# Two tile sizes in the first expert layer: 348 rows, and 294 for what is left of an expert

## The chip, the core and the metric

The program runs on one core of a Trainium2 chip. The core has a matmul engine (TensorE, PE in the rows, with its weight loads as PEld), a vector engine (VectorE, DVE), an activation engine (ScalarE, ACT), a general engine (GpSimd, POOL) and a sequencer that issues most of the transfers (SyncE, SP). The metric is the device time of one execution in microseconds, taken as the median of several runs.

## The reference

Three layers follow one another: a squared-ReLU attention, and two layers in which every row goes through one of eight small networks ("experts"). The change is in the first expert layer. Cut to that:

```python
N, D, E, F = (9984, 256, 8, 1024)
out = x.copy()
xc = x[x @ w_skip > 0]
logits = xc @ w_gate
e_idx = np.argmax(logits, axis=1)
gate_w = softmax(logits)[np.arange(len(xc)), e_idx]
for e in range(E):
    mask = e_idx == e
    h = np.maximum(xc[mask] @ w1[e], 0.0)
    y[mask] = gate_w[mask, None] * (h @ w2[e])
out[do_compute] = xc + y
```

The second expert layer takes all 9984 rows, picks an expert for each in the same way, and has the same two matmuls. The inputs are fixed. Counted with the reference, the experts of the first layer get 628, 689, 640, 488, 610, 684, 607 and 613 rows, 4959 in all; in the second layer two experts get 5042 and 4942.

## The kernel before

**Stages.** The attention runs first, up to about 715 us. While it runs, each row of the result is written into the list of its expert in memory, by indirect transfers. Then come the tiles of the first expert layer, about 714 to 1005 us, and those of the second, up to the end. A tile of the first layer is 348 rows of one expert's list, 116 partitions times 3 groups (`P1, G1`, `T1`); one of the second layer is 512 rows.

**A turn.** One tile is worked on in one turn (`Moe.turn`, `Moe.work`). Its PE work is eight steps `h0` to `h7` (`hidden`, L833: six matmuls each, the two weight halves times the two halves of the rows, since every number is split into a high and a low part), and eight steps `o0` to `o7` (`Moe1.out_part`, L939: six matmuls each). After each `h` step ACT makes the high part `hh` (L835) and DVE the low part `hl` (L836); three PSUM buffers `ph` serve the `h` steps in turn. Behind each step hang hooks, by a table named `PLAN`; the order on each engine is the order in which the hooks are written.

**What the hooks do.** Into a turn are woven (a) the loads for the next turn, 2 MB of weights and the rows; (b) the splitting of weights in high and low parts, `w2` by ACT and POOL (L715) at `h2` to `h5`, `w1` by ACT and DVE (`zB`, L717) at `o1` to `o5`; (c) the transposes of the next tile's rows (`x_transposed`, L816, with ACT's `mxh` and DVE's `mxl` L821) at `o0` and `o2`, through one PSUM buffer; (d) the steps of `after`, which finish the tile before: its result is copied out, the gate of the second layer is computed from it (`logits_t` L962 behind `h2`, ACT's copies `mlt` L968, `logits` L988 behind `h4`, the pick of the expert, which ends with the one-hot `ohbb` of L1003), the places in the lists are ranked (`ranks`, L1010, behind `o0`), and the rows are transposed back (L975) and scattered into the lists of the second layer (`m1.send`, L737, on POOL).

**Sixteen turns.** An expert of 488 to 689 rows takes two tiles, so there are sixteen. Turns 1 to 3 are written out and take the first 348 rows of experts 0, 1 and 2, which are full by then. A table then says which expert and which rows each further tile has (`Table.make`, in steps spread over turns 1 and 2; it ends in `spread`, one matmul of `diag` by ones, L650, and three copies of it on DVE). All engines read the count `n`, here 12, from SBUF (`count`, L663) and go into a loop (L1279) of twelve turns; turn 16 is written out behind it and loads for the second layer. At the end of a loop there is a barrier: SP waits for the transfers that the loop issued, POOL gathers, and all engines are released.

## Time and profile before

| | us |
|---|---|
| median of 3 runs | 1476.23 (1475.93 to 1477.01) |
| the profiled execution | 1476.05 |
| its span, first to last instruction | 1474.2 |
| PE busy in the span | 1459.5 |
| granted PE clock, mean | 0.999 of full speed |

The profile is one execution. Times in its rows are microseconds from the span's start; the 1.85 us between the span and the execution's time are outside the instructions. A timeline row gives start, length, engine, line, operation, tiles and shapes, a count where equal instructions were merged, and in brackets how long the engine had been idle before it and what ended that. A length includes the engine's pipeline: matmuls that follow one another at 0.16 us have lengths of 0.32 us. So the pace is read from starts.

### The profile page before, as it was taken

To read this page: it belongs to the slowest core of one execution; us is meant where nothing else is said; L and a number is where in the kernel's file an instruction comes from. 1 tells how busy PE (TensorE), PEld (TensorE's weight loads), DVE (VectorE), ACT (ScalarE), POOL (GpSimd) and SP (SyncE) were. 2 spreads that over 40 slices of the span, in tenths; PEclk is the share of its full clock that TensorE was granted. 3 is DMA by queue.
4 is the path that set the end of the run, shared out by engine and by line. 5 is a ranking of instruction groups with operands and counts; after the bars stand their busy time and mean duration, and the time that the engine had idled before them with its cause. 6 is when DMAs were issued, how large, how long until landed. Compare 5 with 4: busy or idle time off the path is not lost. (4 is left out here: it accounts for less than half of the span.)

```text
span 1474.2 us, 35153 instructions
## 1 busy us (share of the span) xinstructions
PE 1459.5 (99%) x10985; PEld 1263.7 (86%) x10985; DVE 1070.8 (73%) x2540; ACT 946.6 (64%) x1721; POOL 509.8 (35%) x788
## 2 busy tenths in 40 slices
PE   9999999999999999999999999999999999999998
PEld 7988888888888888888889999998888888888886
DVE  8888888888888888787887777777555555555553
ACT  8877777777777787776556666654554545545453
POOL 2011111111111111111356556655535445354454
PEclk9999999999999999999999999999999999999999
DMA  6411211112111140011345655554433344334440
GB/s 231 180 41 56 80 38 42 44 59 73 37 43 44 58 145 31 29 61 45 99 140 182 184 185 179 180 173 131 172 133 129 132 153 140 132 129 132 154 140 28
DMA packets 46370, 161.00 MB, mean 109 GB/s; under 512 B 12118, under 2 KB 12821, under 8 KB 37056
## 3 DMA queue, kind: packets, MB, share of 16 engines
q1 hardware_dynamic: 29232, 124.57, 26.0%
q0 software_dynamic: 16896, 35.11, 6.8%
q8 instruction: 62, 1.02, 0.3%
q14 instruction: 36, 0.29, 0.1%
q10 hardware_dynamic: 144, 0.02, 0.0%
HBM read 124.57 MB, written 36.21 MB: 109 GB/s over the span
## 5 line engine op out<-in xcount | busy, mean ns | idle before, releaser
L350 PE MATMUL o<-ah,vh 64*128 64x512 f32 (+1 forms) x1560 | 313.6, 384 | 0.1
L350 PE MATMUL o<-al,vh 64*128 64x512 f32 (+1 forms) x1560 | 306.8, 383 | 0.0
L350 PE MATMUL o<-ah,vl 64*128 64x512 f32 (+1 forms) x1560 | 304.9, 382 | 0.0
L836 DVE SCALAR_TENSOR_TENSOR hl<-ph,hh 128x512 fp32r<-128x512 f32 (+1 forms) x288 | 176.3, 613 | 146.3 <-ACT hh L835 138.6
L715 POOL TENSOR_TENSOR w<-w2raw,w 128x256 fp32r<-128x256 f32 x282 | 198.5, 744 | 211.1 <-issue 188.4
L737 POOL DMA_INDIRECT lists<-r,ix x80 | 102.0, 1275 | 476.5 <-ACT t L310 246.5
L312 DVE TENSOR_TENSOR al<-t,ah 128x1024 fp32r<-128x1024 f32 (+2 forms) x201 | 239.9, 1193 | 19.0
L298 ACT ACTIVATE t<-s 128x1024 f32<-128x1024 f32 (+2 forms) x201 | 201.2, 1002 | 79.5 <-PE s L295 71.8
L835 ACT ACTIVATE hh<-ph 128x512 fp32r<-128x512 f32 (+1 forms) x288 | 155.6, 540 | 100.3 <-PE ph L833 92.7
L833 PE MATMUL ph<-mxh,zA 128*128 128x512 f32 (+1 forms) x576 | 209.3, 363 | 3.1 <-DVE hl L836 1.6
L310 ACT ACTIVATE t<-t 128x1024 f32<-128x1024 f32 (+2 forms) x201 | 208.1, 1036 | 5.7
L833 PE MATMUL ph<-mxh,zB 128*128 128x512 f32 (+1 forms) x576 | 207.0, 359 | 0.0
L833 PE MATMUL ph<-mxl,zA 128*128 128x512 f32 (+1 forms) x576 | 206.8, 359 | 0.0
L311 DVE CAST ah<-t 128x1024 fp32r<-128x1024 f32 (+2 forms) x201 | 136.9, 681 | 63.0 <-ACT t L310 59.7
L350 PEld LDWEIGHTS o<-ah,vh 64*128 64x128 f32 x1560 | 153.9, 184 | 28.0 <-DVE xs L363 0.5
L350 PEld LDWEIGHTS o<-al,vh 64*128 64x128 f32 x1560 | 154.0, 184 | 25.9 <-DVE al L312 0.2
L350 PEld LDWEIGHTS o<-ah,vl 64*128 64x128 f32 x1560 | 150.4, 184 | 25.9
L939 PE MATMUL o<-hh,w 128*128 128x348 f32 x512 | 124.8, 327 | 0.0
L833 PEld LDWEIGHTS ph<-mxh,zA 128*128 128x128 f32 x576 | 108.4, 188 | 19.0 <-DVE hl L836 3.1
L820 ACT CAST mxh<-m 128x512 fp32r<-128x512 f32 (+1 forms) x72 | 37.9, 526 | 134.6 <-PE m L816 83.4
L295 PE MATMUL s<-zA,zB 64*128 64x512 f32 (+1 forms) x400 | 123.9, 386 | 0.0
L295 PE MATMUL s<-zB,zA 64*128 64x512 f32 (+1 forms) x400 | 121.6, 387 | 0.0
(240 smaller groups left out, 3012.8 us busy)
## 6 DMA issues: line engine op xcount, KB each, us to landing
w1raw<-in_w SPq DMA_DIRECT2D x36, 1024.0 KB
w2raw<-in_w SPq DMA_DIRECT2D x36, 1024.0 KB
x_in<-lists SPq DMA_DIRECT2D x20, 536.0 KB
vraw<-in_v SPq DMA_DIRECT2D x20, 512.0 KB
ut<-in_uT SPq DMA_DIRECT2D x20, 512.0 KB
lists<-x_in POOLq DMA_DIRECT2D x16, 536.0 KB
x_cur<-lists SPq DMA_DIRECT2D x16, 351.8 KB
x_in<-lists SPq DMA_DIRECT2D x15, 351.8 KB
```

The lines of the kernel that those rows point to most:

```text
L295: nc.tensor.matmul(s[:, i, :n], w[p, k], x[p, q], start=(j == 0), stop=(j == 2))
L298: nc.scalar.activation(t[:, i, :n], s[:, i, :n], AF.Relu, scale=SCALE)
L310: nc.scalar.activation(t[:, i, :n], t[:, i, :n], AF.Square)
L311: nc.vector.tensor_copy(h[:, i, :n], t[:, i, :n])
L312: nc.vector.tensor_tensor(l[:, i, :n], t[:, i, :n], h[:, i, :n].bitcast(F32), op=ALU.subtract)
L350: nc.tensor.matmul(o[half][d][:, :n], w[p, d * 128:d * 128 + 128], x[p, :n], start=(u == 0 and j == at[0]), stop=(u == 9 and j == at[-1]),)
L715: lo_engine.tensor_tensor(l[:, c], src[:, c], h[:, c].bitcast(F32), op=ALU.subtract)
L737: i = tc.nc.gpsimd.indirect_dma_start(out=out, out_offset=bass.IndirectOffsetOnAxis(ap=ix, axis=0), in_=rows, in_offset=None, bounds_check ...
L833: nc.tensor.matmul(ps, w, x, start=(i == 0), stop=(i == len(mms) - 1))
L835: nc.scalar.activation(h, ps, AF.Relu)
L836: nc.vector.scalar_tensor_tensor(l, ps, 0.0, h.bitcast(F32), op0=ALU.max, op1=ALU.subtract)
L939: nc.tensor.matmul(self.y[d], w[:, dd], h[f], start=(f == 0 and i == 0), stop=(f == 7 and i == 2))
```

## The change

There is a third tile size, `P3 = 98` partitions times 3 groups, `T3 = 294` rows. The main table counts a tile of 348 only where more than 294 rows are left after the tiles before it. With the counts above, that is ten tiles of 348 (three of them in turns 1 to 3), and six of 294, for experts 0, 2, 3, 4, 6 and 7 (280, 292, 140, 262, 259 and 265 rows left); experts 1 and 5 have two of 348. A second object `s1`, which shares the tiles of `m1`, works the small tiles. It has a table of its own, made in eight hooks of turn 3 (`step3`, and the `spread` at `o7`). The first loop then has six turns, and behind it stand a written-out turn of 348, a written-out turn of 294, a second loop of four turns of 294, and a written-out turn of 294. There are still sixteen turns, and the weights are still loaded sixteen times. In `Scatter.group` the small POOL instruction ahead of a transfer reads another column.

```diff
+P3 = 98
+T1, T2, T3 = P1 * G1, P2 * G2, P3 * G1
...
+    def rest(self, nc, pool, k, m):
+        lists, self.T = self.lists, T3
+        self.lists = pool.tile([128, 5 * E + 1], F32, name=f"plan_lists{m}")
+        done = pool.tile([128, E], F32, name=f"done{m}")
+        nc.vector.tensor_scalar(done, self.nt, float(T1), None, op0=ALU.mult)
+        nc.vector.tensor_tensor(self.lists[:, 0:E], lists[:, 0:E], done, op=ALU.add)
+        nc.vector.tensor_copy(self.lists[:, E:3 * E], lists[:, E:3 * E])
+        yield
+        yield from self.make(nc, pool, k, lists[:, 3 * E:4 * E], done, None, m, T3, 0, 1, 2.0)
...
+    tiles = {T1: -(-N // T1), T2: -(-N // T2), T3: 1}
+    for T, least in ((T1, T3), (T2, 0), (T3, 0)):
+        k.steps[T] = const.tile([128, tiles[T]], F32, name=f"steps{T}")
+        iota(k.steps[T], tiles[T], T, least)
...
+    t3 = s1.table.rest(nc, sh.p, k, 3)
+    step3 = (lambda: next(t3, None),)
+    m1.turn(lambda: m1.next(-1), m1.after(plan.lim[:, 0, :, 1:2], lambda: 2 * N), {
+        **{at: [*hs] for at, hs in m1.PLAN.items()},
+        ("h", 2): [*m1.PLAN["h", 2], step3],
+        ("h", 3): [*m1.PLAN["h", 3], step3],
+        ("h", 7): [*m1.PLAN["h", 7], step3],
+        ("o", 3): [step3],
+        ("o", 4): [*m1.PLAN["o", 4], step3],
+        ("o", 5): [*m1.PLAN["o", 5], step3],
+        ("o", 6): [step3],
+        ("o", 7): [(lambda: s1.table.spread(nc, sh.ps_m, k),)],
+    })
     n = m1.table.count(nc)
     with tc.For_i(0, n, 1, iteration_sync=mode, head_align_engines=(mybir.EngineType.PE,)) as j:
         m1.send()
         m1.turn(lambda: m1.next(j), m1.finish(j))
     m1.send()
+    m1.turn(lambda: s1.next(-1), m1.finish(n))
+    m1.send()
+    last = m1.after(m1.table.lim[:, :, ds(n + m1.table.S, 1)], lambda: s1.table.row(nc, 0, T3), then=s1)
+    s1.turn(lambda: s1.next(0), last)
+    m1.send()
+    n = s1.table.count(nc)
+    with tc.For_i(0, n, 1, iteration_sync=mode, head_align_engines=(mybir.EngineType.PE,)) as j:
+        s1.send()
+        s1.turn(lambda: s1.next(j + 1), s1.finish(j + 1))
+    s1.send()
...
-    m1.turn(lambda: (m2, e2, ra), m1.finish(n))
+    s1.turn(lambda: (m2, e2, ra), s1.finish(n + 1))
```

On DVE, in turn 3 from `h2` to `h5`, this stands before the change (`hl` are the low parts of `h3`, `h4` and `h5`, L988 is the gate's logits):

```order
L966 COPY mlt<-m 16x116
L836 SCALAR_TENSOR_TENSOR hl_10867<-ph,hh_10859 128x348
L836 SCALAR_TENSOR_TENSOR hl_10868<-ph,hh_10860 128x348
L988 SCALAR_TENSOR_TENSOR m<-m,x_cur 116x8 x3
L836 SCALAR_TENSOR_TENSOR hl_10869<-ph,hh_10861 128x348
```

After the change the same stretch reads so (L602 to L625 are the first two steps of the new table):

```order
L988 COPY mlt<-m 16x116
L602 TENSOR_SCALAR done_11561<-nt_11201 128x8
L603 TENSOR_TENSOR plan_lists_11560<-plan_lists,done_11561 128x8
L604 COPY plan_lists_11560<-plan_lists 128x16
L851 SCALAR_TENSOR_TENSOR hl_10869<-ph,hh_10861 128x348
L621 TENSOR_TENSOR plan_lists_11560<-plan_lists,done_11561 128x8
L624 TENSOR_TENSOR over_11578<-plan_lists_11560,steps_107 128x8
L625 TENSOR_REDUCE nt_11579<-over_11578 128x8
L851 SCALAR_TENSOR_TENSOR hl_10870<-ph,hh_10862 128x348
L1010 SCALAR_TENSOR_TENSOR m<-m,x_cur 116x8 x3
L851 SCALAR_TENSOR_TENSOR hl_10871<-ph,hh_10863 128x348
```

Three small instructions stand ahead of the low part of `h3` and three ahead of that of `h4`.

On PE, at the end of turn 3 (the last matmuls of `o7`, the read of the count, the branch into the loop, the first matmul of `h0`), this stands before the change:

```order
L939 MATMUL o_10883<-hl_10871,w_10855 128x348
L663 TENSOR_LOAD n_i_11428
L1279 COMPARE_AND_BRANCH
L1279 ISA
L1279 UNCONDITIONAL_BRANCH
L1370 BRANCH_PREFETCH_HINT
L833 MATMUL ph<-mxh,zA_114 128x348
```

and this after it:

```order
L961 MATMUL o_10885<-hl_10873,w_10857 128x348
L665 MATMUL m<-diag_11753,ones_f 128x90
L678 TENSOR_LOAD n_i_11436
L1317 COMPARE_AND_BRANCH
L1317 ISA
L1317 UNCONDITIONAL_BRANCH
L1418 BRANCH_PREFETCH_HINT
L848 MATMUL ph<-mxh,zA_116 128x348
```

The matmul of the new table's `spread` stands between the last output matmul and the loop.

On PE, in the loop's turn behind `o2` (transposes back of the third group, then the second half of the next tile's rows), this stands before the change:

```order
L939 MATMUL o_10883<-hl_10866,w_10853 128x348
L975 ISA
L975 MATMUL m<-ident,yS 116x128 x2
L816 REGISTER_ALU
L816 MATMUL m<-ident,x_in 128x116 x3
L939 MATMUL o_10882<-hh_10859,w_10853 128x348
```

and this in the second loop after it:

```order
L961 MATMUL o_10885<-hl_10868,w_10855 128x294
L997 ISA
L997 MATMUL m<-ident,yS 98x128 x2
L831 REGISTER_ALU
L831 MATMUL m<-ident,x_in 128x98 x3
L961 MATMUL o_10884<-hh_10861,w_10855 128x294
```

Order and number of instructions are the same; the shapes are smaller.

## Rows read from the trace of the kernel before

**Rows 1.** The page: busy time of each engine, share of the span, instructions.

```profile
PE 1459.5 (99%) x10985; PEld 1263.7 (86%) x10985; DVE 1070.8 (73%) x2540; ACT 946.6 (64%) x1721; POOL 509.8 (35%) x788
```

**Rows 2.** Timeline of PE: first and last of runs of equal matmuls.

```profile
862.32 0.32 PE L833 MATMUL ph<-mxh,zA 128*128 128x348 f32 x1
...
865.02 0.33 PE L833 MATMUL ph<-mxh,zB 128*128 128x348 f32 x1
...
1239.70 0.39 PE L833 MATMUL ph<-mxh,zA 128*128 128x512 f32 x1
...
1248.99 0.40 PE L833 MATMUL ph<-mxh,zB 128*128 128x512 f32 x1
1249.23 0.39 PE L1107 MATMUL o<-w,hh 128*128 128x512 f32 x1
...
1253.04 0.40 PE L1107 MATMUL m<-w,hh 128*128 128x512 f32 x1
```

**Rows 3.** Timeline of PE in a turn of the loop, which starts at 862.32.

```profile
871.73 0.19 PE L1010 MATMUL m<-ohbb,tri 116*128 116x32 bf16 x1
...
874.83 0.52 PE L816 MATMUL m<-ident,x_in 116*128 116x116 f32 x3
...
879.94 0.32 PE L833 MATMUL ph<-mxh,zA 128*128 128x348 f32 x1
```

**Rows 4.** Timeline of ACT in that turn.

```profile
866.08 0.51 ACT L968 COPY mlt<-m 16x116 f32<-16x116 f32 x2
...
868.04 0.46 ACT L835 ACTIVATE hh<-ph 128x348 fp32r<-128x348 f32 x1
```

**Rows 5.** Timeline of DVE in that turn.

```profile
868.61 0.52 DVE L836 SCALAR_TENSOR_TENSOR hl<-ph,hh 128x348 fp32r<-128x348 f32 x1 [0.39 <-ACT hh L835]
...
871.31 0.18 DVE L1003 TENSOR_TENSOR ohbb<-m,mk 116x24 bf16<-116x24 f32 x1
...
874.26 0.51 DVE L821 TENSOR_TENSOR mxl<-m,mxh 128x348 fp32r<-128x348 f32 x1
```

**Rows 6.** The loop's end: timeline of PE, and SP's waits (total us, times, longest).

```profile
985.48 0.32 PE L939 MATMUL o<-hl,w 128*128 128x348 f32 x1
986.54 0.40 PE L833 MATMUL ph<-mxh,zA 128*128 128x348 f32 x1 [0.73 <-PEq L1370]
...
SPq L1279 <- DMA w2raw<-in_w: 1.6, 1, 1.6
```

**Rows 7.** Timeline of turn 2: its first matmul, POOL and DVE, turn 3's first.

```profile
735.58 0.32 PE L833 MATMUL ph<-mxh,zA 128*128 128x348 f32 x1
...
742.63 4.18 POOL L715 TENSOR_TENSOR w<-w2raw,w 128x256 fp32r<-128x256 f32 x6 [1.97 <-ACT w L712]
743.42 0.68 DVE L622 TENSOR_TENSOR w<-plan_lists,hot 128x40 f32<-128x40 f32 x1
...
756.38 0.32 PE L833 MATMUL ph<-mxh,zA 128*128 128x348 f32 x1
```

**Rows 8.** Timeline of DVE: the second layer's table, eleven instructions from first to last.

```profile
1027.62 0.20 DVE L622 TENSOR_TENSOR w<-plan_lists,hot 128x40 f32<-128x40 f32 x1
...
1029.44 0.37 DVE L639 TENSOR_TENSOR diag<-ident,val 128x204 f32<-128x204 f32 x1
```

**Rows 9.** Timeline of turn 3 and the loop's start: POOL, DVE and PE.

```profile
761.35 5.61 POOL L715 TENSOR_TENSOR w<-w2raw,w 128x256 fp32r<-128x256 f32 x8 [3.49 <-ACT w L712]
...
761.66 0.52 DVE L836 SCALAR_TENSOR_TENSOR hl<-ph,hh 128x348 fp32r<-128x348 f32 x1 [0.73 <-ACT hh L835]
762.53 0.52 DVE L836 SCALAR_TENSOR_TENSOR hl<-ph,hh 128x348 fp32r<-128x348 f32 x1 [0.35 <-ACT hh L835]
...
768.84 0.52 PE L816 MATMUL m<-ident,x_in 116*128 116x116 f32 x3
...
773.73 0.06 DVE L995 MEMSET mk_drop<- 116x3 f32 x1 [1.11 <-DVEq L1279]
...
773.96 0.34 PE L833 MATMUL ph<-mxh,zA 128*128 128x348 f32 x1
```

74 lines of the change are left out of this document (40 added, 34 removed).

## The prediction

> **What bounds the kernel now.** I read the page first: PE is busy 1459.5 us, 99% of the span [rows 1], so a gain has to be a shorter PE stream, and a wait that is put on PE costs its whole length. Then the timeline of PE for its pace. From 862.32 to 865.02 lie 17 matmuls of 348 columns, 0.1588 us each; from 1239.70 to 1248.99 lie 41 of 512 columns, 0.2266 each; eleven pairs of one 512 and one 256 from 1249.23 to 1253.04 take 0.3464, so 256 columns take 0.120 [rows 2]. The three lie on a line of 0.00042 us a column. Then one turn of the loop, 862.32 to 879.94: 17.62 us [rows 2, 3], with no idle time on PE in it. Last, the other engines of that turn, to see how late they may come before PE waits. Two places are tight. The ranking matmul L1010 starts at 871.73, and what it needs, `ohbb`, starts at 871.31 and takes 0.18. The second transposes of the next rows start at 874.83, and what they need, the low part `mxl` which frees their one buffer, runs from 874.26 for 0.51 [rows 3, 5]: 0.06 later, so these matmuls start when DVE lets them.
>
> **What the change removes.** Six of the sixteen turns get 294 columns for 348. On the line of [rows 2] a matmul of 294 takes 0.136, so 0.0228 less. A turn has 96 such matmuls and four of the gate's: 2.28 us, and some 0.05 from narrower transposes: 2.33 us a turn, 14.0 in six. That is the gain if no engine but PE matters.
>
> **What stays of it in a small turn.** The small DVE and ACT instructions of the gate do not shrink, so their chain moves up less than PE does; I follow it from the turn's start.
> - The first gate copy `mlt` on ACT starts at 3.76 (866.08 [rows 4]). It follows PE's first 22 matmuls: 0.50 earlier, 3.26.
> - ACT then works without a pause to `hh` of `h4`, 1.96 later (868.04 [rows 4]). One `hh` in between is shorter by 0.04: 5.18. Its low part starts 0.57 after it (868.61), now 0.53: 5.71.
> - From there DVE has no pause to `ohbb`, 2.70 later (871.31 [rows 5]). Two `hl` in it lose 0.055 each (1.0 ns a column, from the 0.17 us by which the lengths at 512 and 348 columns differ): 8.30. With its 0.18 and the 0.06 of a hand-over, L1010 can start at 8.54. PE would be there at 9.41 less 58 matmuls' 1.32: 8.09. It waits 0.45.
> - DVE goes on to `mxl`, 2.95 later (874.26 [rows 5]), 2.84 with two shorter `hl`; with 0.46 of its own and 0.06 the second transposes start at 11.66. PE, from 8.54, would be there 3.10 less 0.30 later, at 11.34. It waits 0.32.
> - From there to the turn's end were 5.11, less 30 matmuls' 0.68 and 0.02: 16.07.
>
> So a turn of the second loop takes 16.07 for 17.62, a gain of 1.55. I take 1.55 for four turns, 1.45 for the first small turn, whose gate is still that of a tile of 348 (four matmuls), 1.4 for the last, whose transposes are the second layer's wider ones, and 0.1 for the narrower gate in the second layer's first turn: 9.15 us.
>
> **What the change adds.** First, a second loop. At the first one's end PE's last matmul starts at 985.48 and the next at 986.54: without the barrier it would be 985.64, so 0.90 us. SP's wait for `w2raw` ended before PE did [rows 6]; in a small turn that transfer is issued with POOL's splits, which hang on ACT's chain and so move up about 0.5 against 1.55 for PE. I take 0.9, with 2.0 as the far end. At its start PE has no gap (773.96 follows the pace, [rows 9]): 0.1. The transfers, with two more loads written out, stay behind other work: their count does not change.
>
> Second, the table in turn 3: 25 DVE instructions. Its first three, behind `mlt`, fit into the 0.73 us for which DVE waits ahead of the low part of `h3`. The next three stand ahead of that of `h4`, where it waits 0.35 [rows 9]. POOL is splitting weights at that time, 761.35 to 766.96. In turn 2 an instruction of the same kind took 0.68 while POOL split, and ended when a piece of POOL's work of 0.70 did; in the second layer's table, with POOL idle, it took 0.20 [rows 7, 8]. Of the three, two have two inputs in SBUF: 0.65 + 0.70 + 0.2 = 1.55, so `h4`'s low part comes about 1.1 later (0.1 if POOL does not matter). Behind `hl` of `h7` come two more, 0.5, of which 0.25 goes into an idle stretch. PE feels this at the second transposes, where it has no slack (768.84 [rows 9]): 1.3 us. From `o3` to `o6` DVE gets fourteen more; eleven of this kind took 1.82 us to the last one's start [rows 8], here some 2.7 in all with that last one. DVE had ended 1.4 us before PE at the end of turn 3, as its next instruction at 773.73 came after 1.11 of branching; so the matmul of `spread`, which needs `diag`, makes PE wait about another 1.3, and takes 0.1. Then three copies (0.4 and 0.4 to reach them) and 1.11 of branching until DVE starts on the loop's first turn, about 2 us late against PE. PE meets that at the gate's first matmuls on low parts, which had about 1.0 us of slack: 1.0. The sum is 1.3 + 1.4 + 1.0 = 3.7; I take 3.8. A check is turn 2, which carries the other table and one split of weights on DVE: 20.80 us (735.58 to 756.38 [rows 7]) against 17.58 for turn 3, so 3.2. Bounds: 2.3 if POOL does not delay and the lag at the start is hidden, 5.5 if the engines also wait for DVE's copies before they branch.
>
> **The sum.** 9.15 - 0.9 - 0.1 - 3.8 = 4.35 us. From the profiled execution's 1476.05 that leaves 1471.7; the median of the runs lies 0.2 higher, so **1471.9**.
>
> **The rivals.**
> A. No waits in the small turns: DVE and ACT find time elsewhere in their order. For it speaks that DVE has idle time in each turn (73% busy in the span [rows 1]). Against it is that both places have their slack shown above, 0.24 and none. Then 14.0 - 0.9 - 0.1 - 3.8 = 9.2 us: 1467.
> B. The table and the loop cost their upper ends: 9.15 - 2.0 - 0.1 - 5.5 = 1.55 us: 1474.7, too little to see. For it speaks that all of the table's extra work falls on a turn whose DVE feeds PE directly; against it the 3.2 of turn 2.
> C. Slower: the weight loads set the pace. Each matmul has a load of its own, and PEld is busy 1263.7 us, 86% [rows 1]. If a load and not the columns sets 0.1588, the small turns gain nothing and the costs of 4.8 stand alone: 1481. It decides from the point where a small turn gains less than 4.8 / 6 = 0.8 us. Against it: with a load ahead of each, matmuls of 256 columns run at 0.120 [rows 2].
> The Trainium skill ("Trainium Kernel Development and Optimization", Performance Expectations) holds that the busy share of weight loads is a good measure of how near a kernel is to its limit, and that of matmuls a bad one; by it C would be likely, and the sum 1481. The rows at 256 columns differ, and I go by them.
> D. Every taken branch into and in the new loop costs what the loop's end cost, 0.9: an entry, four ends of turns and the exit, 5.4 for the 1.0 above. The gain is gone: 1476.3. Against it the existing loop: its turns follow one another with no gap (879.94 follows the pace, [rows 3]).
> The Trainium skill ("Runtime: NRT & Kernel Launch", Instruction fetch mechanics) states that a taken branch to a place not held makes the engine fetch before it goes on. That speaks against a second loop. The rows show such a price on PE at the loop's end alone.
> E. The change does less than it says: expert 2 has 292 rows left, two under the bound. If rounding on the chip moved three rows, there would be five small tiles: 1473.4.
>
> **How the numbers follow.** About 0.2% (3 us) is what a measurement of this kernel can tell from no change; that is 1473.3. My forecast has 0.47, with a range of its own of 1470 to 1474 (a part, 0.08, above 1473.3); A 0.18, B 0.20, C 0.07, D 0.05, E 0.03. Faster: 0.39 + 0.18 + 0.03 + a few hundredths of B where only one of its costs is met = 0.63. Within: 0.08 + 0.16 + 0.05, rounded to 0.29. Slower: 0.07 and a hundredth of D: 0.08. The range reaches from A's 1467, less half a microsecond, to 1476, which holds B and leaves C and most of D out.
>
> **What will show it.** Matmuls of 294 columns at 0.136. Turns of the second loop at 16.1 us, with waits of PE at L1032 (for `ohbb`) and at the second transposes (for `mxl`), 0.3 to 0.5 each; at 15.3 us A is right, at 17 or more C. Turn 3 longer by some 2.8 with PE idle ahead of L665, and about 1 lost in the first turn of the loop. A gap of 0.9 at the second loop's end, none at its start. Wrong would be above all a turn 3 that hides its table, or small turns whose chain on ACT and DVE starts from another event than PE's gate matmuls.

## The result, and the profile after

| | before | after |
|---|---|---|
| median, us | 1477.01 (1475.93 to 1478.96) | 1484.48 (1483.2 to 1486.04) |
| the profiled execution | 1476.05 | 1483.2 |
| its span | 1474.2 | 1481.4 |

The ratio is 1.0051 [1.004, 1.0063]: 7.5 us slower, where 4.3 us faster was forecast. The work did shrink. This is the page of after, the busy time of each engine, its share of the span and its instructions, as in [rows 1]:

```profile
PE 1450.6 (98%) x10987; PEld 1248.4 (84%) x10987; DVE 1074.2 (73%) x2567; ACT 941.5 (64%) x1721; POOL 515.7 (35%) x797
```

PE is busy 8.9 us less and the span is 7.2 longer, so some 16 us of idle time on PE are new. In the changed kernel the lines have moved: the `h` matmuls are L848 (L833 before), the `o` matmuls L961 (L939), the ranks L1032 (L1010), the second transposes L831 with `mxl` L836 (L816, L821), the second layer's gate L984 (L962), ACT's copies of the finished tile `yS`, `yh` L975, L976 (L953, L954), DVE's `yl` L979 (L957), the scatter L752 (L737). The loops begin at L1317 and L1327.

The table of stretches of after, cut at the first matmul of each turn (length; busy time of each engine with its instructions; granted clock; DMA share, GB/s). They are turn 3, the first loop's first turn, the first small turn up to the second loop's first matmul, that loop's four turns, and the last small turn:

```profile
756.24:778.52 22.28, 18.97 (x122) 17.37 (x121) 17.57 (x66) 11.20 (x28) 8.09 (x15) 1.00 0.47 146
778.52:796.73 18.21, 17.86 (x118) 17.15 (x119) 15.08 (x48) 10.07 (x24) 12.93 (x20) 1.00 0.55 175
902.72:922.04 19.32, 16.00 (x120) 14.99 (x119) 12.93 (x42) 11.07 (x29) 13.84 (x21) 1.00 0.55 171
922.04:939.87 17.83, 17.39 (x118) 16.33 (x119) 12.76 (x44) 8.83 (x22) 12.38 (x23) 0.90 0.55 165
939.87:957.91 18.04, 16.02 (x120) 14.83 (x119) 12.75 (x44) 9.72 (x25) 10.54 (x18) 1.00 0.55 171
957.91:975.84 17.93, 15.99 (x121) 14.80 (x119) 12.67 (x44) 9.75 (x25) 10.14 (x18) 1.00 0.52 167
975.84:995.24 19.40, 16.15 (x121) 14.76 (x119) 12.11 (x40) 9.75 (x25) 7.52 (x13) 1.00 0.47 147
995.24:1012.22 16.98, 16.10 (x121) 15.26 (x121) 13.82 (x48) 10.46 (x26) 12.53 (x23) 1.00 0.61 197
```

Against the forecast, stretch by stretch:

| stretch | before | forecast | after | off by |
|---|---|---|---|---|
| turn 3 and the loop's first turn | 35.48 | 39.28 | 40.49 | +1.2 |
| six more turns of 348, the first loop's end | | 106.6 | 105.99 | -0.6 |
| first small turn, second loop's start | | 16.27 | 19.32 | +3.0 |
| four turns of the second loop, its end | | 65.18 | 73.20 | +8.0 |
| last small turn | | 16.22 | 16.98 | +0.8 |

PE is busy for 16.0 to 16.2 us in the small turns (17.39 in the one at 922.04, where PE's clock is halved for a while, as shown below), near the 16.07 that were forecast for a whole turn; the stretches take up to 19.4, so the rest is waiting. This is what PE waits for between 714 and 1020 us (total, times, longest), first after, then before:

```profile
PE m L831 <- DVE mxl L836: 3.2, 8, 0.8
PE ph L848 <- DVE mk_hi L858: 3.1, 1, 3.1
PE m L984 <- DVE yl L979: 2.3, 3, 0.8
PE ph L848 <- ACT yh L976: 2.2, 1, 2.2
PE ph L848 <- DVE hl L851: 2.1, 4, 1.0
PE ph L848 <- PEq L1418: 2.0, 2, 1.3
PE m L984 <- ACT yh L976: 2.0, 3, 0.7
PE m L1032 <- DVE ohbb L1025: 1.2, 5, 0.3
PE m L665 <- DVE n_i L655: 0.7, 1, 0.7
```

```profile
PE ph L833 <- DVE hl L836: 1.6, 2, 1.0
PE m L816 <- DVE mxl L821: 1.1, 2, 0.8
PE ph L833 <- PEq L1370: 0.7, 1, 0.7
...
PE m L1010 <- DVE ohbb L1003: 0.2, 1, 0.2
```

The waits forecast are there. `mxl` is up by 2.1 over the six small turns, about as forecast (0.32 each); `ohbb` by 1.0, where 0.45 each would be 2.7; PE's sequencer at the loops' ends by 1.3. Four were not forecast or not in that size: 3.1 (`mk_hi`) at the second loop's start, 2.2 (`yh`, line L848) at the first loop's start, and 2.3 and 2.0 (`yl`, `yh`) at the gate L984, three times each.

**The two starts.** The timeline of PE after turn 3, then of PE and DVE at the second loop's start:

```profile
775.82 0.46 PE L665 MATMUL m<-diag,ones_f 128*128 128x90 f32 x2 [0.72 <-DVE n_i L655]
778.52 0.40 PE L848 MATMUL ph<-mxh,zA 128*128 128x348 f32 x1 [2.25 <-ACT yh L976]
```

```profile
921.05 0.06 DVE L1017 MEMSET mk_drop<- 98x3 f32 x1 [2.99 <-issue]
...
922.04 0.37 PE L848 MATMUL ph<-mxh,zA 128*128 128x294 f32 x1 [3.09 <-DVE mk_hi L858]
```

At the first start PE has nothing queued behind the matmul of `spread`, and the read of the count and the branch, which before ran beside the last `o7` matmuls (no gap in [rows 9]), lie open: PE idles for 2.25. The second start has no such wait ahead of it. `mk_hi` can't be what held PE: DVE itself stood still for 2.99 and waited for nothing that the profile shows. The branches of the sequencers into the loops (ns; then the start) show where the time went, first at L1317, then at L1327:

```profile
L1317 PEldq COMPARE_BRANCH  x1: 400/400/400, 777.7 to 777.7; - x1
```

```profile
L1327 PEldq COMPARE_BRANCH  x1: 4157/4157/4157, 917.4 to 917.4; - x1
...
L1327 DVEq COMPARE_BRANCH  x1: 89/89/89, 920.6 to 920.6; - x1
```

The same instruction takes 0.40 us into the first loop and 4.16 into the second. In that stretch (916.5 to 922.2) the DMA queues (packets, MB, share of 16 engines) list packets of the kind "instruction":

```profile
q1 hardware_dynamic: 160, 0.54, 29.8%
...
q14 instruction: 4, 0.03, 2.0%
q8 instruction: 1, 0.02, 1.7%
```

At the first start, 771 to 779, there is one. Afterwards the clock falls: with 1.6 us of work behind that gap, PE is granted 0.50 of full speed (1.2 GHz for 2.4) for 3.4 us. This is that stretch, in the columns of the table above:

```profile
923.64:927.05 3.41, 3.41 (x16) 3.01 (x15) 1.77 (x4) 1.12 (x4) 2.91 (x5) 0.50 0.86 224
```

That half clock costs 1.7, which is what the turn of 17.83 is over the others' 16.1 without waits.

**The gate's waits.** Timeline of the turn that starts at 957.91: POOL's scatters, ACT's copies of the finished tile, PE's gate matmuls:

```profile
955.98 0.98 POOL L752 DMA_INDIRECT lists<-x_out,ix_scatter1s  x1 [0.60 <-issue]
...
957.53 0.97 POOL L752 DMA_INDIRECT lists<-x_out,ix_scatter1s  x1 [0.18 <-issue]
...
958.88 0.98 POOL L752 DMA_INDIRECT lists<-x_out,ix_scatter1s  x1 [0.18 <-issue]
```

```profile
958.20 0.41 ACT L975 COPY yS<-o 128x294 f32<-128x294 f32 x1 [2.19 <-PE o L961]
...
960.46 0.41 ACT L975 COPY yS<-o 128x294 f32<-128x294 f32 x1 [1.55 <-PE ph L848]
```

```profile
961.22 0.31 PE L984 MATMUL m<-yh,wg_split 128*16 128x294 f32 x1 [0.60 <-ACT yh L976]
...
962.42 0.31 PE L984 MATMUL m<-yl,wg_split 128*16 128x294 f32 x1 [0.75 <-DVE yl L979]
```

ACT's second copy stands 2.26 behind the first and is put down to a matmul of `ph`. What it needs is in the PSUM buffer since the end of the turn before; its semaphore counts PE's matmuls. In the events of this trace, PE's counts come 0.69 to 0.77 us apart around this place, where PE issues a matmul every 0.134: at 956.58, 957.26, 958.02, 958.78, 959.55 and 960.31, and then nineteen within 0.65 us. So the matmuls are done and their counts are held up; ACT is told late, and `yh` and `yl` are late for the gate.

My theory from these rows: three independent costs, (1) the table in turn 3, which leaves PE's queue empty at the first loop, (2) a stop at the second loop's start for code not yet held, with the half clock behind it, (3) counts that come late while POOL issues the scatter, which the shorter turn brings nearer to the gate. The rivals: the small tile's columns don't pay (C); the table's DVE work and not its place costs; the stop is a collision with transfers; the gate's waits come from the smaller tile's chain itself.

The last clause of (3) does not hold. In the first loop of this trace the scatters stand at nearly the same places (in the turn at 831.75 the second starts 0.38 ahead of the first matmul, as here, and the third 1.48 behind it for 0.97 here). There the counts have only single gaps of 0.47 to 0.80, ACT's second copy comes 0.69 behind the first, and PE does not wait. The kernel before shows the same gaps in its loop. So late counts were there before the change and cost nothing; why they pile up in the second loop is not shown.

### The profile page after: what moved, and what is told of

Same layout as the page of the kernel before. It is cut to its first block, busy times and chain, and to the rows that moved or that the text cites. A ratio compares the mean times of both kernels' runs of the same rounds, so it can differ in the third digit from the quotient of the medians.

```text
span 1481.4 us, 34886 instructions
## 1 busy us (share of the span) xinstructions
PE 1450.6 (98%) x10987; PEld 1248.4 (84%) x10987; DVE 1074.2 (73%) x2567; ACT 941.5 (64%) x1721; POOL 515.7 (35%) x797
## 5 line engine op out<-in xcount | busy, mean ns | idle before, releaser
L851 DVE SCALAR_TENSOR_TENSOR hl<-ph,hh 128x512 fp32r<-128x512 f32 (+2 forms) x288 | 173.6, 604 | 149.3 <-ACT hh L850 144.8
L752 POOL DMA_INDIRECT lists<-r,ix x80 | 103.1, 1289 | 476.7 <-ACT t L311 246.1
L848 PE MATMUL ph<-mxh,zA 128*128 128x512 f32 (+2 forms) x576 | 208.1, 361 | 10.1 <-DVE mk_hi L858 3.1
L850 ACT ACTIVATE hh<-ph 128x512 fp32r<-128x512 f32 (+2 forms) x288 | 152.8, 533 | 101.1 <-PE ph L848 95.9
L848 PE MATMUL ph<-mxl,zA 128*128 128x512 f32 (+2 forms) x576 | 205.2, 356 | 0.0
L848 PE MATMUL ph<-mxh,zB 128*128 128x512 f32 (+2 forms) x576 | 205.1, 356 | 0.0
L848 PEld LDWEIGHTS ph<-mxh,zA 128*128 128x128 f32 x576 | 108.7, 189 | 26.6 <-issue 9.5
L835 ACT CAST mxh<-m 128x512 fp32r<-128x512 f32 (+2 forms) x72 | 37.4, 519 | 135.7 <-PE m L831 74.7
L1130 PE MATMUL o<-w,hh 128*128 128x512 f32 x320 | 120.5, 405 | 0.0
```

The lines of the kernel that those rows point to most:

```text
L752: i = tc.nc.gpsimd.indirect_dma_start(out=out, out_offset=bass.IndirectOffsetOnAxis(ap=ix, axis=0), in_=rows, in_offset=None, bounds_check ...
L848: nc.tensor.matmul(ps, w, x, start=(i == 0), stop=(i == len(mms) - 1))
L850: nc.scalar.activation(h, ps, AF.Relu)
L851: nc.vector.scalar_tensor_tensor(l, ps, 0.0, h.bitcast(F32), op0=ALU.max, op1=ALU.subtract)
L1130: nc.tensor.matmul(self.y[g][:P], self.hh[f][:, gg], w.rearrange("p t d -> p (t d)"), start=(f == 0), stop=False)
```

## The experiments

Diffs are against the changed kernel, and `...` marks what is left out of them. Ratios are times against the kernel before on the same chip, so that more than 1 is slower. The chips differ in one respect (late counts), so their numbers are given.

**The second loop written out** (four turns as they stand, which is right for these inputs only).

```diff
-    n = s1.table.count(nc)
-    with tc.For_i(0, n, 1, iteration_sync=mode, head_align_engines=(mybir.EngineType.PE,)) as j:
+    n = 4
+    for j in range(n):
```

> The four turns of the second loop are written out one after another (their number is fixed at 4, so this form is only right for these inputs). Theory, loop entry: of the changed kernel's 1484.5, the second loop's start costs 3.1 us of PE, because PE's branch into it took 4.16 us while it waited for code, the stretch of 3.4 us at half clock that follows costs 1.7, and the loop's end 1.3: without the loop all 6.1 go. If PE's waits at L984 (1.5 us in each of three turns) belong to the scatter or to the small tile itself they stay, and the time is 1478.4 or a little more; if they belong to the loop, 4.5 more go: 1473.9. Rival, data: PE waits at the loop's start for a result of DVE (mk_hi) that is late for its own reasons, and only the end's 1.3 goes: 1483.2.

1474.39 against 1476.57, ratio 0.9986 [0.9976, 0.9996], on chip 12. The six small turns take 16.07, 16.71, 16.11, 16.27, 16.87 and 16.51; ACT's second copy comes 0.60 behind the first in each. So the loop, not the tile, made the turns of 18 us: 10 us lie between the two medians. One more difference between the two forms stands in the traces. In a turn of the loop nearly every matmul of PE adds to its semaphore (117 of 118 in the turn at 957.91 of after), in a written-out turn of this run (952.38) 29 of 118 do. Whether that is why written-out turns are free of the late counts was not tried. Rival C falls here: 96 matmuls of 294 columns pay as the line of [rows 2] said. The table still costs its five (22.29, then a first loop turn of 19.15 with a stretch at half clock).

**The scatter held back** to the `h1` step of the next turn, in the second loop.

```diff
-        s1.send()
-        s1.turn(lambda: s1.next(j + 1), s1.finish(j + 1))
+        s1.turn(lambda: s1.next(j + 1), s1.finish(j + 1), {
+            **s1.PLAN,
+            ("h", 1): [(lambda: s1.sc.touch(s1.sc.spare, *[s1.hl[1][:, 0:1].bitcast(F32)] * 2),), (s1.send,)],
+        })
```

> In the second loop the scatter of a tile's rows on POOL is held back until hl of step 1 of the next turn is there, some 2.6 us after that turn's start; in the changed kernel it runs from 1.9 us before to 1.9 us after the start. Theory, scatter: while POOL issues the scatter, PE's semaphore counts come through one in 0.76 us, so ACT's second yS copy (wait for PE ph, 1.5 us) is late and PE waits at L984 for yh and yl. Then ACT's wait ahead of the second yS and PE's waits at L984 go (4.5 us in all); the slow counts move to 2.6 to 6.6 us after the start, and PE waits for hl at L848 there instead, or POOL's low halves of w2 come late: between 1480 and 1486. Rival, small tile: ACT and DVE are too slow for 294 columns in any case, the waits at L984 stay at 1.5 us a turn and the time is 1484.5 or more.

1486.68, ratio 1.007 [1.0053, 1.0087], chip 12. Timeline of the turn that starts at 958.69, ACT's two copies and the first scatter:

```profile
958.63 0.41 ACT L975 COPY yS<-o 128x294 f32<-128x294 f32 x1 [1.84 <-PE o L961]
...
959.23 0.43 ACT L975 COPY yS<-o 128x294 f32<-128x294 f32 x1
...
963.41 0.98 POOL L752 DMA_INDIRECT lists<-x_out,ix_scatter1s  x1 [0.46 <-issue]
```

With the scatter away the copies are 0.60 apart and the gate's waits are gone. The late counts went with the scatter: they now lie from 963.68 on. So the scatter's place makes them on this chip. The time was lost again elsewhere: POOL does the scatter where it would split `w2`, PE waits 1.4 to 1.6 for `w` in each turn (the two in the middle take 17.42 and 17.27), and at the loop's end it stands 3.72.

**The spread later**, in the turn behind the first loop, so that nothing waits at the end of turn 3.

```diff
-        ("o", 7): [(lambda: s1.table.spread(nc, sh.ps_m, k),)],
...
-    m1.turn(lambda: s1.next(-1), m1.finish(n))
+    m1.turn(lambda: s1.next(-1), m1.finish(n), {
+        **m1.PLAN,
+        "start": [("after",)],
+        ("h", 0): [("after",), (lambda: s1.table.spread(nc, sh.ps_m, k),), ("next",)],
+    })
```

> The second table's spread (the matmul of L665 and its three copies) moves from the end of turn 3 to the start of the turn behind the first loop; the table's steps stay in turn 3. Theory, preamble: PE's matmul at the end of turn 3 waits 0.72 us for DVE, and then PE's sequencer runs the first loop's preamble (six semaphore waits, a load of the count, a branch: 2.25 us of idle PE) with nothing queued ahead, where before it ran under the last matmuls of the turn. Without the spread in that place both go, 3.0 us: 1481.5. Rival, DVE late: DVE is behind by the table's steps and PE waits for it at the loop's start anyhow; the 0.7 alone goes: 1483.8.

1483.9, ratio 1.005 [1.0033, 1.0067], chip 12. Turn 3 is 20.65, the loop's first 19.31 with 1.79 at its start (now for DVE's own branch) and 1.36 at `mxl`: 39.96 for the two, where after has 40.49 (neither has half clock there). Moving the wait alone gains half a microsecond; DVE is late by then anyway. Here the rival was mostly right: the table's DVE work in turn 3 costs, not only its last step.

**Tiles of 342 rows for 294**, so that the matmuls hardly shrink and the rest of the change stays.

```diff
-P3 = 98
+P3 = 114
```

> The second size is 342 rows (3 x 114) for 294, with all else as in the changed kernel: the gain by columns is nearly gone (0.27 us a turn), and the table, the second loop and its start and end stay; there are eight large and eight small tiles, four turns in the first loop and six in the second. Theory: the costs stand as measured, table 5.0, second loop's start 3.1, half clock 1.7, its end 0.9 (against none before), less 8 x 0.27: 1477.0 + 8.5 = 1485.5, with no waits at L984, because in a turn of 17.3 us the scatter lies earlier. Rival, the second loop as such makes the waits at L984, 1.5 in each of five turns: 1493. Rival, the start's 3.1 and the half clock came from where its transfers fell and are gone here: 1480.7.

Eight of the sixteen tiles are small then, six of them in the second loop. 1489.2, ratio 1.0088 [1.0063, 1.0112], chip 12. That is 4.0 to 4.7 us more than the medians of after (1485.19 on this chip, 1484.48), where 48 columns in 600 matmuls are 12.1 by the line of [rows 2]. So the columns count, but less than half of them reach the end: turns of the second loop are 17.9 to 18.45, and PE waits at L984 for `yl` 0.7 in two of them, so that the narrow tile's waits take up the rest. The time lies between theory and rival, and bears out neither. The start costs 2.22 here. The late counts are there with these tiles too, so it is not the narrow tile that makes them.

**The table moved** into an additional written-out turn of 348 behind the first loop, its steps at `o3` to `o6`, its spread in the next turn; the loop runs once less, and turn 3 has the hooks of before.

```diff
-        ("o", 7): [(lambda: s1.table.spread(nc, sh.ps_m, k),)],
+        **m1.PLAN,
...
-    m1.turn(lambda: s1.next(-1), m1.finish(n))
+    m1.turn(lambda: m1.next(n), m1.finish(n), {
+        **m1.PLAN,
+        ("o", 3): [step3, step3],
+        ("o", 4): [*m1.PLAN["o", 4], step3, step3],
+        ("o", 5): [*m1.PLAN["o", 5], step3, step3],
+        ("o", 6): [step3],
+    })
+    m1.send()
+    m1.turn(lambda: s1.next(-1), m1.finish(n + 1), {
+        **m1.PLAN,
+        "start": [("after",)],
+        ("h", 0): [("after",), (lambda: s1.table.spread(nc, sh.ps_m, k),), ("next",)],
+    })
```

> The second table leaves turn 3, which is as before the change again. One turn more of 348 rows is taken out of the first loop's end and written behind it; the table's seven steps stand at the end of that turn (hidden parts done, output parts 3 to 6, where DVE is idle for some 2.8 us), and the spread at the start of the next. Theory: the table cost 5.0 us because turn 3's DVE has to be done early for the loop's preamble; a turn with a plain turn behind it takes it for 0.5 at most. Then turn 3 is 17.6 long and has no idle PE at the loop's start, and the time is 1484.5 - 4.5 = 1480. Rival: the steps cost the same wherever they stand, because DVE's work there has no slack: 1484.

1473.59 against 1475.38, ratio 0.9986 [0.9976, 0.9996], on chip 3. Turn 3 and the first loop turn take 17.51 and 17.95, as before the change: 5.0 less than with the table there. The steps' turn is 17.61, so they cost nothing in it; the spread's is 19.31, 1.7 too long. The time is some 6 us better than was expected, for two reasons that the edit did not aim at. First, the stop at the second loop's start is gone; PE's branch there, and the next turn's `mxl` and ranks in the second layer, are these:

```profile
L1331 PEldq COMPARE_BRANCH  x1: 351/351/351, 913.4 to 913.4; - x1
```

```profile
1019.80 0.69 DVE L836 TENSOR_TENSOR mxl<-m,mxh 128x512 fp32r<-128x512 f32 x1 [3.80 <-issue]
...
1020.55 0.18 PE L1032 MATMUL m<-ohbb,tri 98*128 98x32 bf16 x1 [2.75 <-DVE mxl L836]
```

The stop now falls on DVE in written-out code, where nothing branches, and half clock follows. Second, on this chip the loop's second and third turn take 16.30 and 16.21 and ACT's copies are 0.60 apart, with POOL's scatters at the same places of the turn (the second 0.38 before its first matmul, the third 0.97 behind it, as in after):

```profile
962.27 0.98 POOL L752 DMA_INDIRECT lists<-x_out,ix_scatter1s  x1 [0.61 <-issue]
...
963.83 0.97 POOL L752 DMA_INDIRECT lists<-x_out,ix_scatter1s  x1 [0.18 <-issue]
```

```profile
964.14 0.41 ACT L975 COPY yS<-o 128x294 f32<-128x294 f32 x1 [1.84 <-PE o L961]
...
964.74 0.42 ACT L975 COPY yS<-o 128x294 f32<-128x294 f32 x1
```

**The scatter held only to `h0`.** The group is issued behind the low part of `h0`.

```diff
+    def send_held(self):
+        self.sc.touch(self.sc.spare, *[self.hl[0][:, 0:1].bitcast(F32)] * 2)
+        for g in range(self.G):
+            self.sc.group(self.rows, self.x_out[:self.P], RW, g)
...
-        s1.send()
-        s1.turn(lambda: s1.next(j + 1), s1.finish(j + 1))
+        s1.sc.ready()
+        s1.turn(lambda: s1.next(j + 1), s1.finish(j + 1), {
+            **s1.PLAN,
+            ("h", 0): [*s1.PLAN["h", 0], (s1.send_held,)],
+        })
```

> As the run with the scatter held back, but its first two small instructions run at once, and the scatter is held for hl of step 0 and not of step 1, so that it starts some 2.7 us after the turn's start, not 4.7, and POOL comes to the low halves of w2 nearly 2 us earlier. Theory, scatter: no waits at L984, and the wait of 1.54 us for POOL's w falls under 0.5: turns of 16.2, 1484.5 - 3 x 1.5 = 1480 with the waits at the loop's start and end as they fall. Rival: the slow counts now meet ACT's hh of steps 2 to 5, and PE waits for hl at L848 as long as before at L984: 1484.5.

1481.37, ratio 1.0044 [1.0028, 1.0061], chip 3. The turns are 16.30, 16.29, 16.50 and 21.18: the last one holds 4.63 at the loop's end. The start costs 2.88. As chip 3 has no late counts, this says nothing on them; it shows the price of a POOL that is late for a barrier.

**Two splits of `w2` moved from POOL to DVE** in the turn ahead of the second loop, so that the load is issued earlier and is over at the loop's start.

```diff
-    s1.turn(lambda: s1.next(0), last)
+    s1.turn(lambda: s1.next(0), last, {
+        **s1.PLAN,
+        ("h", 2): [("after",), w2_dve(0)],
+        ("h", 4): [w2_dve(2), ("after",)],
+    })
```

> In the written turn ahead of the second loop, two of the four low halves of w2 go from POOL to DVE, so that the raw buffer is free some 2.8 us earlier and the next load of 1 MB is over before PE branches into the loop. Theory, collision: PE's branch took 4.16 us because the code had to come through DMA engines that were 90% busy with that load; with the load gone by then the branch takes under 2 us, PE idles under 1.5 at the loop's start for 3.1, and no stretch at half clock follows: 1484.5 - 1.6 - 1.7 = 1481.2, plus up to 0.7 for DVE's added work. Rival: the branch waits for its code for as long whatever else moves (or for data): idle 2.2 to 3.1, 1484.5.

1478.33, ratio 1.0021 [1.0011, 1.003], chip 3. The load of weights is over by 917 and a smaller one by 919.7; PE's branch, which begins at 919.3, still takes 3.52, with 2.40 of idle time and half clock behind it. In the run with the table moved the branch took 0.35 while the transfer engines were 80 to 90% busy. A collision with the loads is not what stops it. The loop's turns without that are 16.22 and 16.21. This kernel is after but for those splits, and has no late counts: table and start alone still make it 3 us slower than before.

**No aligned head** at the second loop, which moves its code and nothing else (one run).

```diff
-    with tc.For_i(0, n, 1, iteration_sync=mode, head_align_engines=(mybir.EngineType.PE,)) as j:
+    with tc.For_i(0, n, 1, iteration_sync=mode) as j:
```

> The second loop's first instruction on PE is not aligned any more. If the padding ahead of the aligned place is what lies outside the code that PE holds, the branch into the loop falls from 4.16 us to about the 0.4 of the first loop, and PE's idle time there from 3.1 to about 0.3: 1480. If not, branch and time stay: 1484.5. The turns inside the loop may grow if PE then has to cross one more block of code in each.

1476.17 on chip 3. PE's branch takes 0.35 and PE has no gap at the start; now only DVE is late (its branch stands at 921.0, 3.8 behind PE's), and PE waits for `yl` 1.54 and 0.44 in that turn, 19.52 with the half clock. The later turns are 16.26, 16.27 and 17.52.

**A turn of 348 written out, the table left in turn 3.**

```diff
...
-    m1.turn(lambda: s1.next(-1), m1.finish(n))
+    m1.turn(lambda: m1.next(n), m1.finish(n))
     m1.send()
+    m1.turn(lambda: s1.next(-1), m1.finish(n + 1))
+    m1.send()
...
```

> The changed kernel with one turn of 348 rows taken out of the first loop's end and written behind it, and nothing else: the table stays in turn 3. This moves the code of all that follows by one turn on every engine. Theory, code: an engine stops for some 2 to 4 us where the program runs straight into code that it has not got yet, and where that is follows from the code's position alone. Then the 3.1 us at the second loop's start go, as in the run with the table moved, DVE stops in the first turn of the second layer instead (2.75 us of PE), and turn 3 still costs 5.0: 1478 to 1482. Rival, table: it was the table in turn 3 that made both, and the second loop's start costs 3.1 again: 1484.

1486.0, ratio 1.0064 [1.0048, 1.0081], chip 1. The start's stop is gone (the turn ahead is 16.06) although its work is the same, which speaks for the place in the code. A stop of 2.05 is now in the second layer at 1040, and the first loop turn is 19.16 with half clock behind the same 2.25. The small loop turns have the gate's waits again (18.19, 17.95, 19.05), so that the time is over the 1478 to 1482 of the theory.

**Table moved, spread at `h2`, no aligned head.** Beside the edits of the table moved:

```diff
+        ("h", 2): [(lambda: s1.table.spread(nc, sh.ps_m, k),), ("next",), *m1.PLAN["h", 2]],
...
-    with tc.For_i(0, n, 1, iteration_sync=mode, head_align_engines=(mybir.EngineType.PE,)) as j:
+    with tc.For_i(0, n, 1, iteration_sync=mode) as j:
```

> The table behind the first loop as in the run with the table moved, its spread two hidden parts later (so that PE no longer waits 1.35 us for DVE), and the second loop without the aligned head. Theory, table: the turn with the spread falls from 19.3 to 17.8, and against 1473.6 the time is 1472.2, if no engine's stop for code moves into the path by the new positions; with one such stop more or less (2 to 3 us, and 1.7 for half clock behind it) it is between 1468 and 1476. Rival: the wait at the spread was cover for something later, and the turn stays at 19: 1473.6.

1480.95, ratio 1.0039 [1.0025, 1.0053], chip 1. The loop's turns, 17.55, 18.21, 17.84 and 19.51, carry the gate's waits of this chip, and the second layer's first turn a stop of 2.39. The time is over the range that was expected. The spread's turn is 18.77, 0.5 better than at `h0`.

**The same with the second loop written out** (for these inputs only).

```diff
+    n = 4
+    for j in range(n):
```

> The table behind the first loop, the spread two hidden parts later, and the four turns of the second loop written out (right only for these inputs): none of the three costs that I found is left, neither the table's 5.0, nor the second loop's start and end, nor the waits at L984. Theory: what is left is the gain by columns less the small tile's own waits, 1474.4 (written out alone) - 4.5 = 1469.9; a stop for code in a new place may add 2 to 4. Rival: the small tile itself gains less than its matmuls show, and the time does not come under 1473.

1470.14 against 1476.35, ratio 0.9962 [0.9947, 0.9976], chip 1, as the one ahead, from which it differs by the loop alone: 10.8 us. Small turns of 16.07, 16.86, 15.96, 15.93, 16.13 and 16.58. The second one has a wait of 1.28 for POOL's split of `w2`, and the spread's turn is still 1.1 too long (18.72). With these, and without the loop's costs and the table's in turn 3, the narrow tiles give 6.2 us.

**Three small turns written out, and a loop for what is left** (here one turn), with the moved table and its spread at `h2`. The loop still takes its count at run time.

```diff
+    for i in range(3):
+        s1.send()
+        s1.turn(lambda: s1.next(i + 1), s1.finish(i + 1))
     n = s1.table.count(nc)
...
-        s1.turn(lambda: s1.next(j + 1), s1.finish(j + 1))
+        s1.turn(lambda: s1.next(j + 4), s1.finish(j + 4))
```

> The table behind the first loop, and of the second loop's four turns three written out, so that the loop runs once here (and as often as other inputs need; a turn without rows changes nothing). Theory: the waits at L984 came from the second turn of that loop on, so none is left; a loop's start and end are, 0.9 for the end and 0 to 3 for the start by where its code falls: 1470.1 + 0.9 to 3.9 = 1471 to 1474, under the kernel before (1476.4) on a chip with slow counts too. Rival: stops for code at the start, at the end and in the second layer's first turn add up to 5 and more with the half clock that follows: 1476 or more.

1470.05 against 1475.32, ratio 0.9966 [0.9954, 0.9979], chip 0. The table of stretches, the first five small turns and the last (columns as above):

```profile
898.80:914.84 16.04, 15.79 (x120) 14.99 (x119) 13.68 (x45) 9.88 (x26) 12.17 (x19) 1.00 0.64 196
914.84:931.53 16.69, 15.44 (x120) 14.81 (x119) 11.93 (x40) 9.73 (x26) 13.63 (x25) 1.00 0.47 142
931.53:947.54 16.01, 15.77 (x120) 14.93 (x119) 13.93 (x50) 9.76 (x26) 11.96 (x18) 1.00 0.72 239
947.54:963.52 15.98, 15.67 (x120) 14.94 (x119) 12.45 (x42) 9.76 (x26) 8.90 (x17) 1.00 0.62 191
963.52:981.19 17.67, 15.63 (x120) 14.69 (x119) 12.59 (x41) 9.76 (x25) 9.02 (x15) 1.00 0.52 167
981.19:998.13 16.94, 15.95 (x120) 15.22 (x121) 14.21 (x49) 10.35 (x26) 12.72 (x23) 1.00 0.65 198
```

The fifth holds the loop's end, 1.4. No turn has half clock, and the loop starts without a stop.

**That kernel again, on chip 12**, unchanged.

> The kernel with three turns written out and the table behind the first loop, on one chip more. Theory: its second loop runs once, so the slow counts can reach no turn but that one and its next; it is at 1470 to 1471.5 on either sort of chip. Rival: with slow counts it loses the 1.4 to 3 us that the loop's one turn and the first loop's lateness bring: 1473.

1474.66 against 1477.81, ratio 0.9981 [0.9972, 0.9991]. The written-out turns agree (16.06, 16.80, 15.93, 15.94); the one turn in the loop is 19.82 for 17.67, with PE's counts 0.67 to 0.76 apart at its start and a wait of 1.55 in the gate (`mlt`). So the same program has late counts on one chip and none on another, and among its small turns only the looped one pays, 2.1.

**That kernel with no aligned head at the second loop.**

```diff
-    with tc.For_i(0, n, 1, iteration_sync=mode, head_align_engines=(mybir.EngineType.PE,)) as j:
+    with tc.For_i(0, n, 1, iteration_sync=mode) as j:
```

> The same with the second loop's head not aligned. Theory, code position: PE does not stop at the loop's start (branch of 0.35 us); another engine may, whose stop reaches PE later or not at all: 1470.1 + 0.9 to 2.5 = 1471 to 1472.6. Rival: alignment makes no difference for a loop that runs once; the time is that of the aligned one within 0.5.

1476.82, ratio 1.0007 [0.9998, 1.0017], chip 0. That is 6.8 us more for a shift of code, and neither theory nor rival had it. One stop of 4.18, where 0.70 is usual, stands in the timeline of PE behind the second layer's loop, with half clock after it, together 5.2:

```profile
1444.08 0.79 PE L848 MATMUL ph<-mxh,zA 128*128 128x512 f32 x1 [4.18 <-issue]
```

**The table moved, again, on chip 0.** The kernel with the spread at `h0`, unchanged.

> The kernel with the table moved once more, on another chip. Theory, chip: on a chip where PE's counts come slowly beside a scatter its second loop has the waits at L984 (1.4 us in each of three turns) that it lacked, and loses some 1.5 more where POOL's and DVE's work comes late: 1473.6 + 1.0 (the chip's kernel before is slower by that) + 4.2 + 1.5 = 1479 to 1480. Where the counts come on time it is 1473.6 again. Rival: it is 1474.5 on any chip, and the waits come from the position of the code.

1474.37, ratio 0.9992 [0.9982, 1.0001]. No late counts, loop turns of 16.87, 16.37, 16.26 and 17.41, and the stop in the second layer's first turn (2.41) again: it belongs to the program, not to the chip.

**The changed kernel again, on chips 1, 12 and 13.**

> The changed kernel once more, on another chip than in its first profile. In that profile (and in the one of the kernel before, from the same chip) the counts of PE's semaphore came slowly while POOL issued a scatter, and the waits at L984 (1.5 us in each of three turns) followed; in the kernels with the table moved, the earlier load and the unaligned loop, with the scatter in the same place of the turn, the counts came on time in every loop and the waits were absent. Theory, chip: the slow counts belong to where a kernel ran and not to the kernel; on a chip where the others have none the waits are absent here too, and the time is 1480 against 1475.4 for the kernel before; turn 3 (22.3) and the second loop's start (3.1, and half clock after it) stay. Rival, kernel: the waits are the changed kernel's own, and it is at 1484 again.

> The changed kernel on one chip more. Theory, chip: where PE's counts come on time beside a scatter it has no waits at L984 and takes 1479 to 1480 (it was 1484.5 and 1484.8 where they came slowly), with 22.3 us for turn 3 and 2.9 to 3.1 of idle PE at the second loop's start as before; where they come slowly it is 1484.5 again. Rival, kernel: 1484.5 with the waits, also where the counts are on time in the first loop.

> The changed kernel once more: so far all its profiles come from chips on which the counts of PE's semaphore came slowly beside a scatter, in its first loop too. Theory, chip: where they come on time in its first loop, its second loop has no waits at L984, the turns there are 16.2 to 16.4 long, and it takes 1479 to 1480. Rival, kernel: the waits at L984 are there with counts on time in the first loop, and it takes 1484.5.

1484.8, 1485.19 and 1483.09; ratios 1.0058 [1.0041, 1.0075], 1.0044 [1.0027, 1.0061] and 1.0047 [1.003, 1.0064]. On all three, PE waits 2.7 to 3.0 at the second start, and six times at L984, 3.6 to 4.2 in all. It has not been seen on a chip with timely counts, so theory and rival are not told apart by these runs, and how much it would lose there is not measured; the kernel with two splits moved, 1.0021 on chip 3, is the nearest.

## Why the prediction was wrong

- **The gain was there.** Matmuls of 294 columns follow one another at 0.134 to 0.137, forecast 0.136. A small turn's chain was right as well: written-out turns take 15.9 to 16.1 where nothing else falls into them, forecast 16.07, with 0.1 to 0.3 at L1032 and 0.1 to 0.3 at the second transposes (forecast 0.45 and 0.32); looped ones without late counts 16.2 to 16.3. Of the gain of 9.15 some is missing: all six written out take 98.54 (loop written out) or 97.53 (with the table moved as well), where 96.67 were forecast, so 0.9 to 1.9 less. It is lost in the second one (16.7 to 16.9), where PE waits 1.25 to 1.28 for POOL's split of `w2`, a wait that the prediction did not have; in the last (16.5 to 16.6); and without the table moved in one turn of 16.87, with a wait of 0.76 at the gate. A's turns of 15.3 are not seen.
- **C** is refuted by these turns; that its 1481 is the rival's time nearest to the measured one is luck. By the Trainium skill ("Trainium Kernel Development and Optimization", Performance Expectations) the busy share of the weight loads is a good measure of how near a kernel is to its limit. The section does not say that the loads set the pace, which is what the prediction made of it; with loads busy 86% before and 84% after, fewer columns did shorten the turn.
- **The table in turn 3: 3.8 was forecast, 5.0 came**, inside the bounds (5.9 to 7.0 in the runs with half clock behind the first start, outside them). The term at the second transposes was right: PE is 1.1 behind the turn of before from `o3` on, for 1.3. The step that failed is "about another 1.3" at `spread`: 3.6 came there for 1.4. PE waits 0.72 for DVE, and behind it the loop's preamble, 2.25, has no matmuls left to hide under; the third term, 1.0 in the loop's first turn, was then 0.3. The place of the wait is not the whole of it, though. With the spread moved away, PE waits 1.79 at the same start for DVE's branch and 1.36 at the second transposes, and only 0.5 of the 5.0 is gained: DVE's lateness costs wherever PE meets it.
- **The second loop's start: 0.1 was forecast, 3.0 more came, and 1.7 of half clock.** The step that failed took the first loop's start, [rows 9], as the price of any start. The kernel with the turn written out (16.06) shows that the same start can be free, so the row held for one place and not for every loop's start. D came nearest: it put a price on branches, but 0.9 on each one, and on every turn, where it is not (0.22 us for the branch back, and no gap). The Trainium skill ("Runtime: NRT & Kernel Launch", Instruction fetch mechanics) has a taken branch to code not held stall an engine, and the sequential crossing of a block "mostly hidden". The stop of 4.16 at a branch agrees in kind with the first; if DVE's stop of 3.80 in straight code is such a crossing, which no run shows, the second does not hold here.
- **The small turns in the loop: 16.07 was forecast, 17.9 to 18.0 came.** The chain that I followed began with `mlt`, which follows PE's first 22 matmuls. It left out the step ahead of it, ACT's two copies and the gate's four matmuls, which before had slack and whose releases I took as prompt. On the chips on which the counts come late this costs 1.7 in each of three turns, 5.1 (17.93 and 18.04 against 16.2 to 16.3): 1.35 to 1.47 as idle time of PE, the rest as its emptied pipeline. The prediction named this as the thing to go wrong ("a chain that starts from another event than PE's gate matmuls") and gave it no price.
- **The loop's end: 0.9 was forecast**, and PE idles 1.28 there, 0.5 more with its pipeline, inside the bounds. **The last turn: 0.8 over**, as the waits at L1032 and the transposes were 0.34 and 0.51 there.

Together: 1.2 for the table, 3.0 and 1.7 at the start, 5.1 at the gate, 0.7 for four looped turns of 16.25 instead of 16.07, 0.5 and 0.8 at the end, less 0.6 in the turns of 348: 12.4, the last column of the table above. The stretches were to take 243.55 for the 248.14 of before, 4.6 less; they took 255.98, 7.8 more, and 0.6 of that came back outside them: 7.2 in the span. The range held neither the start nor the late counts: the start was priced by the one row that showed it free, and the counts had no price.

## What is shown, and what stays open

Shown: the loop and not the tile makes turns of 18 us; the late counts go where the scatter goes (moved on chip 12 alone), and are there on chips 1, 12 and 13 and not on 0 and 3; the stops move when the code is shifted, and one stayed when the loads were moved; the table's place in turn 3 costs 5.0, and 1.1 to 1.7 in a later turn.

Argued only: that the stops are waits for code. Instruction packets stand beside them, and POOL's scatter, which runs beside the stop at the second loop's start, does not run beside the stops of 3.80 and 4.18. But the start without a stop (the table moved) has four instruction packets too, from 914.4 to 917.2.

Open: which position of the code is free and which is not; why POOL's indirect transfers delay PE's counts on some chips, where the traces also hold fewer count events (105 to 113 for a turn of PE, about 120 on the others); and why they cost a wait in the second loop and none in the first.

The version with three small turns written out and the table in a later turn is faster than both kernels: 0.34% faster than before on chip 0 and 0.19% on chip 12.

## What to carry to other kernels

A shorter tile on the bounding engine pays its columns, but each runtime loop that it needs has a start and an end of its own. The end left PE idle for 0.7 to 1.7 us in most runs, and for 3.7 to 4.6 where POOL was late; the start cost nothing at one position in the program and 4.7 with the half clock at another. So give a new loop's start a range of that width, and do not price it by the existing loop. Put work that PE has to wait for where matmuls are still queued behind it, and leave the engine that feeds PE time to catch up ahead of a loop: moving the wait alone gave 0.5 us, moving the whole table 3.3 to 3.9. When a turn is shortened, follow the chain from its very first release, and ask which waits depend on a count that is given while another engine issues indirect transfers.

## What the chip showed that was not expected

- An engine can stop for 2 to 4 us with nothing to wait for: at a loop's start (PE's branch 4.16 for 0.35 to 0.40), behind a loop (4.18) and in straight code (3.80 on DVE).
- In the second loop PE's semaphore counts come 0.67 to 0.77 us apart beside POOL's indirect scatters on chips 1, 12 and 13, with a matmul issued every 0.134, and then in a burst 0.03 to 0.04 apart; on chips 0 and 3 each matmul's count comes on time.
- After these gaps PE often runs for 3.4 us at 1.2 GHz. Behind the second loop's start that cost 1.7. The first loop's start with 2.25 of idle time had it in some runs (first turn 19.15) and not in others (18.21), and the second layer's stop of 2.39 did not have it.
